# Attention and a gated MLP on one core: output transfers moved from SyncE's queue to ScalarE's, and one block of the attention matrix turned by VectorE only from the ninth pair on

## The chip, the cores and the metric

The kernel runs on one core of a Trainium2 chip. The metric is the device time of one execution in microseconds. A core has five engines, each with its own queue that is worked off in order: TensorE (PE in the profile; its weight loads are listed as PEld), VectorE (DVE), ScalarE (ACT), GpSimd (POOL) and SyncE (SP), which here only issues transfers. A transfer can be issued by SP or by ACT; it then runs beside the engines, and those who need it wait for a semaphore.

## The reference

Eight batches of eight heads, sequence 576, head size 64: causal attention with a decay per position, and behind it an MLP with a spatial gate.

```python
scores = scale * np.matmul(q, k.transpose(0, 1, 3, 2))
decay = cum[:, :, :, None] - cum[:, :, None, :]
scores = np.where(causal, -1000000000.0, scores + decay)
scores = scores - np.max(scores, axis=-1, keepdims=True)
attn = np.exp(scores)
attn = attn / (np.sum(attn, axis=-1, keepdims=True) + 1e-09)
x = np.matmul(attn, v)                      # then heads side by side: (8, 576, 512)
...
h = np.maximum(x @ w_in, 0.0)
u, v = (h[..., :d_ff // 2], h[..., d_ff // 2:])
v_n = (v - mu) / np.sqrt(var + 1e-06)
v_s = np.einsum('ts,bsd->btd', w_spatial, v_n) + b_spatial[None, :, None]
return ((u * v_s) @ w_out).astype(np.float32)
```

## The kernel before, in words

The heads are taken in pairs: 32 pairs P = 0 to 31, four to a batch (PPB = 4). A batch's attention (`attention`, L695) and a batch's MLP (`moe`, L724) are generators; the loop at L854 runs the MLP of batch b beside the attention of batch b + 1 and keeps the two level by the numbers `t_attn` and `t_moe` (L836). Batch 0's attention runs alone at the start, in `first` (L514). A scheduler with a model of time then fixes the order of each engine's queue; on the chip that order is kept.

**A pair.** PE makes the scores against 128 keys at a time (L328). DVE adds the decay and takes the row's minimum (L308), ACT makes the exponentials and their sum (L339), POOL divides by the sum (L316; for pairs 5 to 7 it is ACT, L314). The result is in the tiles `tt`, one per head, queries on the partitions. For the product with v it must stand the other way round, in `e`, in blocks c = 0 to 3 of 128 keys. Blocks 1 to 3 are turned by PE (L413, four, three, two or one pieces of 128 x 128) and copied out of PSUM by DVE and ACT in turn (L404). **Block 0 is moved** (`move`, L442): DVE turns it in pieces of 32 x 32 into `mid` (L449, one instruction per head), and SP issues 16 transfers of 32 KB (L456) that set the pieces on the right partitions of `e`, or of a second tile `ea` for every other pair. The matmuls on such a block (`spread`, L483) read it in its scattered order; the others are L475. Pairs 0 to 3 turn all four blocks on PE; from pair 4 on block 0 is moved.

**The MLP.** Per batch 576 rows: matmuls with w_in, norm, spatial product, gate (L803 to L807), and the last product with w_out in `w_out_tile` (L818): four tiles of 128 rows per batch, two after each half of the sequence, and behind every second batch one tile more with 64 rows of each of two batches. PE makes a tile in 12 matmuls into one of two PSUM buffers `ps`; ACT copies it to the SBUF tile `o` (L831), and it is sent out (L833). There is one buffer `o`: the next copy waits until the transfer before has landed. The first 64-row half of the tile behind every second batch, and all 128-row tiles, go out on SP's queue, the other half on ACT's.

**Loads.** SP also issues the loads: scores' inputs `qk_t` (L239), the decay rows `dk` (L251) and `dt` (L253), `vraw` (L293) for one pair ahead, and in batch 1's stretch the weights `w` in pieces (L125), which ACT, DVE and POOL split into a rounded part and a rest (L130 to L143). POOL masks each `dk` and `dt` after it has landed (L279 to L285).

**Semaphores of transfers.** The framework gives the transfers of both queues eight semaphores in turn (DMAHW0 to DMAHW7 below). A transfer is issued only when the one eight places before it in the program's order has landed, whichever queue that one is on.

Of the kernel before, what the change touches and what calls it, by code (L numbers as in the profile page):

```python
# [22 lines left out]
NB = 4  # L23
# [2 lines left out]
TOFF = (0, 128, 384, 768)  # L26
RSTEP = 384
ROFF = tuple(RSTEP * i for i in range(4))
MOVED = (0,)
HALVES = ((0, 256), (256, 320))  # L30
QK = 640 + S
EOFF = (0, 640, 1280, 1088, 576)


def f32(ap):
    return ap.bitcast(F32)
# [3 lines left out]
def attn_gmlp_kernel(ctx: ExitStack, tc: tile.TileContext, qk, v, f, w_in, w_sp, b_sp, w_out, out):  # L40
# [7 lines left out]
    B = out.shape[0]  # L48
    PPB = NPAIR // B
# [8 lines left out]
    V, A, G, T, SY = nc.vector, nc.scalar, nc.gpsimd, nc.tensor, nc.sync  # L58
# [125 lines left out]
    tt = [cst.tile([128, 3 * RSTEP + TL], F32, name=f"tt{h}") for h in range(2)]  # L184
# [4 lines left out]
    def turn(P):  # L189

        if P not in own:
            own[P] = tt, tl
            if P < PPB and P % 2:
                tl2 = wk.tile([128, 640], F32, name="tl2", tag="xh", bufs=6)
                G.memset(tl2[:, S:640], 0.0)
                own[P] = [ws_[0].tile([128, 1280], F32, name=f"t2{h}", bufs=1) for h in range(2)], tl2
        return own[P]
# [11 lines left out]
    def bank(n, piece=True):  # L209

        t = PS['s'].tile([128, 512], F32, name="sc", tag=f"sc{n}")
        if piece:
            banks.append(n)
        return t

    def in_one_piece(jobs, needs=()):

        was = None
        for job in jobs:
            if was is None:  # L220
                was = job()
                for j in [freed[n] for n in banks if n in freed] + list(needs):
                    behind(was, j, sync=True)
            else:
                with tc.high_priority():
                    i = job()
                behind(i, was)
                was = i
        banks.clear()

    def mm(o, l, r, st, sp):
        T.matmul(o, l, r, start=st, stop=sp)  # L232
# [58 lines left out]
    def prep_v(P):  # L291
        vraw = wk.tile([128, 5, 2, D], F32, name="vraw", tag="vraw")
        SY.dma_start(out=vraw, in_=v[P])  # L293
        vts[P] = vraw
# [96 lines left out]
    def e_tile(P):  # L391
        return e_all

    def e_first(P):

        return aside[P] if P in aside else e_all
# [10 lines left out]
    def turn_block(P, h, c):  # L407

        tt, _ = turn(P)
        n = 512 - 128 * c  # L410
        tp = bank(2 + c, False) if P < PPB and c > 1 else PS['t'].tile([128, 512], F32, name="tp")
        for i in range(c, NB):
            T.transpose(out=tp[:, (i - c) * 128:(i - c + 1) * 128],  # L413
                        in_=tt[h][:, off(P)[i] + 128 * c:off(P)[i] + 128 * c + 128], identity=ident)
        return lambda by=None: evac(P, e_tile(P)[:, h, EOFF[c]:EOFF[c] + n], tp[:, 0:n], by)
# [15 lines left out]

    def transposes(P, h):
        for c in range(NB):
            if c not in MOVED:
                turn_block(P, h, c)()
                yield 107 * (NB - c)

    def part(t, k, steps):

        return bass.AP(tensor=t.tensor, offset=t.offset, ap=[list(t.ap[0]), *steps])  # L440

    def move(P):  # L442

        tt, _ = turn(P)
        for c in MOVED:
            w = 128 - 32 * c
            mid = cst.tile([128, 2, 4, w], F32, name=f"mid{c}", tag=f"mid{c}")
            for h in range(2):
                V.transpose(out=part(mid[:, h], 0, [[32, NB - c], [w, 4], [1, 32]]),  # L449
                            in_=part(tt[h][:, ROFF[c] + 128 * c:], 0, [[RSTEP, NB - c], [32, 4], [1, 32]]))  # L450
            if P % 2:
                aside[P] = cst.tile([128, 2, 512], F32, name="ea")
            e = e_first(P)
            for g in range(4):
                for r in range(4):
                    copied.setdefault(P, []).append(SY.dma_start(  # L456
                        out=e[32 * r:32 * r + 32, :, EOFF[c] + w * g:EOFF[c] + w * g + w],
                        in_=mid[32 * g:32 * g + 32, :, r, :]))

    def transposes_tail(P):  # L460
        for cs, off, step in TAILS:
            turn_tail(P, cs, off, step)()
            yield 107 * len(cs)

    def attend(P, xh, xl):

        vt, e = vts[P], e_tile(P)
        moved = MOVED if P >= PPB else ()
        xb = 4 if P < PPB else 0
        x0, x1 = bank(xb), bank(xb + 1)  # L470
        jobs = []

        def product(x, s0, q0, q1, c, h, end):
            e0 = EOFF[c] - 128 * c
            return lambda: T.matmul(x[64 * h:64 * h + 64, q0 - s0:q1 - s0], vt[:, c, h, :],  # L475
                                    e[:, h, e0 + q0:e0 + q1], start=c == 0 and c not in moved, stop=c == end)

        def spread(x, m0, c, h, end):
            k0 = max(m0, c)
            n, w = m0 + 2 - k0, 128 - 32 * c  # L480
            src = part(e_first(P)[:, h, EOFF[c] + 32 * (k0 - c):], 0, [[w, 4], [32, n], [1, 32]])
            out = part(x[64 * h:64 * h + 64, 128 * (k0 - m0):], 0, [[32, 4], [128, n], [1, 32]])
            return lambda: T.matmul(out, vt[:, c, h, :], src, start=c == 0, stop=c == end)  # L483

        for c in range(NB + 1):
            for x, s0, q0, q1, end in ((x1, 256, max(256, 128 * c), S, NB), (x0, 0, 128 * c, 256, 1)):
                if c > end:
                    continue
                if c in moved:
                    jobs += [spread(x, s0 // 128, c, h, end) for h in range(2)]  # L490
                    if end < NB:
                        continue
                    q0 = TL
                jobs += [product(x, s0, q0, q1, c, h, end) for h in range(2)]
        in_one_piece(jobs, copied.pop(P))
        yield 2950
        for ps, s0, n in ((x0, 0, 256), (x1, 256, 320)):
            last[P, s0 // 256] = A.copy(xh[:, s0:s0 + n], ps[:, 0:n])
        yield 0
        for ps, s0, n in ((x0, 0, 256), (x1, 256, 320)):  # L500
            freed[xb + s0 // 256] = V.tensor_tensor(out=xl[:, s0:s0 + n], in0=ps[:, 0:n], in1=f32(xh[:, s0:s0 + n]),  # L501
                                               op=ALU.subtract)
        yield 0
# [191 lines left out]
    def attention(b):  # L695
        for P in range(b * PPB, (b + 1) * PPB):
            nxt = P + 1 < NPAIR
            prep_v(P)
            if nxt:
                list(prep(P + 1))  # L700
                mask(P + 1)
            if P == PPB:
                move(P)
            for h in range(2):
                yield from transposes(P, h)
            if nxt:
                yield from scores(P + 1)
            yield from transposes_tail(P)
            if nxt:
                yield from scores_tail(P + 1)  # L710
            yield from product(P)
# [106 lines left out]
    def w_out_tile(b, ghi, glo, dst):  # L818
        ps = acc(b)
        n = 0  # L820
        for j in range(NJ):
            for l, r in ((ghi, woh), (ghi, wol), (glo, woh)):
                mm(ps, l[j], r[:, j, :], n == 0, n == 3 * NJ - 1)
                n += 1
            yield 648
        tag, bufs = ("vx", 2) if b == B - 1 and nps[0] % 3 else ("o", 1)
        o = mo.tile([128, DM], F32, name="o", tag=tag, bufs=bufs)
        if b == B - 1 and nps[0] % 3 == 1:
            V.tensor_copy(o, ps)
        else:  # L830
            A.copy(o, ps)  # L831
        for bb, tok, p0, np_ in dst:
            (SY if p0 == 0 else A).dma_start(out=out[bb, tok:tok + np_, :], in_=o[p0:p0 + np_, :])  # L833


    t_attn, t_moe = 33600.0, 52500.0  # L836

    def step(gen, done, t):
        try:
            return done + next(gen) / t, True  # L840
        except StopIteration:
            return round(done), False

    with tc.tile_pool(name="ws", bufs=2) as ws, tc.tile_pool(name="p0s", bufs=1, space=PSUM) as p0s, \
# [4 lines left out]
        da, on = 1.0, False  # L849
# [4 lines left out]
    for b in range(B):  # L854
        gm = moe(b)
        dm, mon = 0.0, True
        while mon:
            while da < min(B, b + 1 + LEAD + dm):
                if not on:
                    gen, on = attention(int(round(da))), True  # L860
                da, on = step(gen, da, t_attn)
            dm, mon = step(gm, dm, t_moe)


# [41 lines left out]
```

## Time and profile before

| | us |
|---|---|
| three runs | 803.22, 805.36, 809.61 (median 805.36) |
| the profiled execution: its time | 804.17 |
| its span, first to last instruction | 802.4 |
| PE busy | 741.0 (92%) |
| DVE busy | 466.6 (58%) |
| ACT busy | 395.3 (49%) |
| POOL busy | 369.1 (46%) |

Mean granted clock of PE over the span: 0.979 of full speed. A busy PE is not a PE at its peak, since matmuls overlap and their ends are modelled; but PE's idle time and what ended it can be read directly. The shares are averages over stages: batch 0's attention alone (to about 74 us), batch 1's attention beside batch 0's MLP (to about 166 us), then six stretches of some 95 us, and the last MLP alone.

### The profile page before, as it was taken

How to read it: one execution, taken by the hardware profiler on the slowest of the kernel's cores; microseconds unless marked ns; L12 is line 12 of the kernel's file. 1: busy time of each engine (PE TensorE's matmuls, PEld its weight loads, DVE VectorE, ACT ScalarE, POOL GpSimd, SP SyncE). 2: the span in 40 equal slices, each digit the busy share in tenths (PEclk: the TensorE clock that was granted, in tenths of full speed). 3: DMA queues.
4: the chain of work that ended last, by engine and by line, in shares of the span. 5: the costliest groups of instructions: out<-in, count | busy, mean ns of one | idle time of the engine just before them, and what ended most of it. 6: DMA issues, size and time to landing. Idle time of an engine off the chain costs nothing.

```text
span 802.4 us, 15003 instructions
## 1 busy us (share of the span) xinstructions
PE 741.0 (92%) x4812; PEld 589.2 (73%) x4813; DVE 466.6 (58%) x1537; ACT 395.3 (49%) x1106; POOL 369.1 (46%) x682
## 2 busy tenths in 40 slices
PE   8778799599999899999899979999889989999997
PEld 4456577477888678886787757977678857888896
DVE  6896898745745457555655527555575535752332
ACT  7855678554644346445544345444364433642331
POOL 3985744454624365433634516344553435531241
PEclk9999999899999999999999989999999999999999
DMA  7746355544325433344233432344433443212001
GB/s 231 219 166 174 85 148 160 154 131 137 106 78 135 132 114 110 120 133 134 73 104 115 134 127 75 106 117 134 150 103 115 112 125 106 81 45 66 27 1 66
DMA packets 70160, 93.21 MB, mean 116 GB/s; under 512 B 11329, under 2 KB 44097, under 8 KB 70082
## 3 DMA queue, kind: packets, MB, share of 16 engines
q1 hardware_dynamic: 69762, 91.74, 38.9%
q8 instruction: 38, 0.62, 0.3%
q10 hardware_dynamic: 320, 0.52, 0.3%
q14 instruction: 40, 0.33, 0.1%
HBM read 67.78 MB, written 9.75 MB: 97 GB/s over the span
## 4 chain that ended last, share of the span: by engine, by line
PE 46%; SPq 10%; POOL 9%; DVE 6%; issue 5%; DMA 5%; ACT 4%; POOLq 0%; ACTq 0%; DVEq 0%
PE ps L232 28%; SPq L456 10%; POOL tt L316 6%; PE sc L328 5%; PE sc L232 4%; DMA out_dram<-o 3%; PE sc L475 3%; PE tp L413 2%; PE tp L232 2%; PE sc L483 2%; DVE tt L308 1%; DVE vx L758 1%; DVE mid L449 1%; DMA dk<-rows_d 1%; PE tp L423 1%
## 5 line engine op out<-in xcount | busy, mean ns | idle before, releaser
L339 ACT ACTIVATE tt<-tt,nm 128x384 f32<-128x384 f32 (+1 forms) x240 | 133.4, 558 | 58.8 <-DVE nm L308 56.7
L807 POOL TENSOR_TENSOR gl<-u,gh 128x256 fp32r<-128x256 f32 (+1 forms) x64 | 51.5, 806 | 162.6 <-ACT gh L806 160.8
L316 POOL TENSOR_SCALAR tt<-tt,sm 128x128 f32<-128x128 f32 x192 | 99.8, 539 | 44.3 <-DVE sm L355 42.8
L308 DVE CUSTOM_DVE_ANT_1 tt<-sc,dk 128x256 f32<-128x256 f32 (+1 forms) x120 | 65.5, 553 | 57.5 <-PE sc L328 40.9
L328 PE MATMUL sc<-qk_t 64*128 64x128 f32 (+3 forms) x512 | 88.5, 465 | 7.9 <-DVE xl L501 5.8
L232 PE MATMUL ps<-xh,winh 128*128 128x256 f32 (+1 forms) x232 | 74.7, 323 | 7.3 <-ACT vx L753 4.8
L475 PEld LDWEIGHTS sc<-e,vraw 128*64 128x64 f32 x784 | 55.6, 138 | 32.4 <-issue 5.7
L232 PE MATMUL ps<-winh,xh 128*128 128x512 f32 x148 | 64.0, 433 | 16.1 <-ACT o L831 15.0
L475 PE MATMUL sc<-e,vraw 128*64 128x320 f32 (+4 forms) x784 | 73.3, 324 | 5.5 <-ACT tl L627 4.3
L232 PE MATMUL ps<-sph,vnh 128*128 128x256 f32 (+1 forms) x240 | 76.6, 319 | 0.0
L404 ACT COPY e<-tp 128x384 f32<-128x384 f32 (+2 forms) x120 | 45.6, 380 | 55.0 <-PE tp L413 24.7
L413 PE MATMUL tp<-ident,tt 128*128 128x128 f32 x364 | 67.4, 280 | 5.2 <-ACT e L404 3.1
L404 DVE COPY e<-tp 128x384 f32<-128x384 f32 (+2 forms) x128 | 57.9, 455 | 22.9 <-PE tp L413 20.6
L232 PE MATMUL ps<-sph,vnl 128*128 128x256 f32 (+1 forms) x240 | 70.6, 294 | 0.0
L232 PE MATMUL ps<-spl,vnh 128*128 128x256 f32 (+1 forms) x240 | 70.6, 294 | 0.0
L232 PE MATMUL ps<-xl,winh 128*128 128x256 f32 (+1 forms) x232 | 69.6, 300 | 0.0
L232 PE MATMUL ps<-xh,winl 128*128 128x256 f32 (+1 forms) x232 | 69.3, 299 | 0.0
L328 PEld LDWEIGHTS sc<-qk_t 64*128 64x128 f32 x512 | 45.5, 191 | 30.9 <-DVE xl L501 7.1
L413 PEld LDWEIGHTS tp<-ident,tt 128*128 128x128 f32 x364 | 46.0, 142 | 25.2 <-issue 4.8
L449 DVE STREAM_TRANSPOSE mid<-tt 128x512 f32<-128x512 f32 x56 | 39.7, 708 | 37.0 <-POOL tt L316 31.1
L232 PE MATMUL ps<-winl,xh 128*128 128x512 f32 x148 | 60.3, 408 | 0.0
L308 DVE CUSTOM_DVE_ANT_0 tt<-sc,dk 128x384 f32<-128x384 f32 (+1 forms) x120 | 49.7, 418 | 10.6 <-PE sc L328 9.6
(218 smaller groups left out, 1818.5 us busy)
## 6 DMA issues: line engine op xcount, KB each, us to landing
qk_t<-in_dram SPq DMA_DIRECT2D x32, 608.0 KB, 5.5
dk<-rows_d SPq DMA_DIRECT2D x58, 320.0 KB, 4.6
vraw<-in_dram SPq DMA_DIRECT2D x32, 320.0 KB, 3.1
dt<-rows_d SPq DMA_DIRECT2D x58, 144.0 KB, 3.2
out_dram<-o SPq DMA_DIRECT2D x32, 256.0 KB, 2.2
e<-mid SPq DMA_DIRECT2D x224, 32.0 KB, 1.9
ea<-mid SPq DMA_DIRECT2D x224, 32.0 KB, 1.9
w<-in_dram SPq DMA_DIRECT2D x16, 256.0 KB, 3.3
```

The lines of the kernel that those rows point to most:

```text
L232: T.matmul(o, l, r, start=st, stop=sp)
L308: return V.tensor_tensor_reduce(out=out, in0=ps, in1=dec, scale=-0.125, scalar=3.0e38, op0=ALU.add, op1=ALU.min, accum_out=acc_)
L316: G.tensor_scalar(out=t, in0=t, scalar1=r, scalar2=1.0, op0=ALU.mult, op1=ALU.mult)
L328: return lambda: T.matmul(ps[:, c:c + n], qk_t[p, n - 128:n], qk_t[p, 640:640 + n], start=True, stop=True)
L339: last["exp", P, h, i] = A.activation(t, t, AF.Exp, bias=nm, scale=-1.0, accum_out=sm)
L404: copied.setdefault(P, []).append(by(out, ps))
L413: T.transpose(out=tp[:, (i - c) * 128:(i - c + 1) * 128], in_=tt[h][:, off(P)[i] + 128 * c:off(P)[i] + 128 * c + 128], identity=ident)
L449: V.transpose(out=part(mid[:, h], 0, [[32, NB - c], [w, 4], [1, 32]]), in_=part(tt[h][:, ROFF[c] + 128 * c:], 0, [[RSTEP, NB - c], [32, 4] ...
L456: copied.setdefault(P, []).append(SY.dma_start(out=e[32 * r:32 * r + 32, :, EOFF[c] + w * g:EOFF[c] + w * g + w], in_=mid[32 * g:32 * g + ...
L475: return lambda: T.matmul(x[64 * h:64 * h + 64, q0 - s0:q1 - s0], vt[:, c, h, :], e[:, h, e0 + q0:e0 + q1], start=c == 0 and c not in move ...
L483: return lambda: T.matmul(out, vt[:, c, h, :], src, start=c == 0, stop=c == end)
L807: G.tensor_tensor(out=gl[j][:, 0:nt], in0=g, in1=f32(gh[j][:, 0:nt]), op=ALU.subtract)
```

## The change

Two things. An output transfer is issued by ACT, in the queue that holds the copy to `o`, except in the last batch, where whole tiles stay on SP. And block 0 is moved only for pairs P >= 8; pairs 4 to 7 turn it on PE, as pairs 0 to 3 do. With that, the second tile `ea` goes to the even pairs and not the odd ones, the first of them being pair 8, and the pacing number of the attention that runs beside batch 0's MLP is 37000 and not 33600.

```diff
-MOVED = (0,)
...
     def transposes(P, h):
         for c in range(NB):
-            if c not in MOVED:
+            if c not in moved(P):
                 turn_block(P, h, c)()
                 yield 107 * (NB - c)
...
+    def moved(P):
+
+        return (0,) if P >= 2 * PPB else ()
...
         tt, _ = turn(P)
-        for c in MOVED:
+        for c in moved(P):
...
-            if P % 2:
+            if P % 2 == 0:
                 aside[P] = cst.tile([128, 2, 512], F32, name="ea")
...
-        moved = MOVED if P >= PPB else ()
+        away = moved(P)
...
-                if c in moved:
+                if c in away:
                     jobs += [spread(x, s0 // 128, c, h, end) for h in range(2)]
...
-            if P == PPB:
-                move(P)
...
         for bb, tok, p0, np_ in dst:
-            (SY if p0 == 0 else A).dma_start(out=out[bb, tok:tok + np_, :], in_=o[p0:p0 + np_, :])
+            (SY if p0 == 0 and b == B - 1 else A).dma_start(out=out[bb, tok:tok + np_, :], in_=o[p0:p0 + np_, :])
...
-    t_attn, t_moe = 33600.0, 52500.0
+    t_first, t_attn, t_moe = 37000.0, 33600.0, 52500.0
...
-                da, on = step(gen, da, t_attn)
+                da, on = step(gen, da, t_attn if b else t_first)
```

The changed kernel's line numbers are one lower than the kernel's before up to L433, and one to three higher behind it.

**ACT's queue at the end of an odd batch (batch 3).** `o<-ps` is the copy of an output tile, `tp` and `xh` belong to the attention beside it; in brackets stands what an instruction waits for by semaphore. Before:

```order
L498 CAST xh<-sc 128x320 [waits PE_49]
L831 COPY o<-ps 128x512 [waits DMAHW0_49,PE_49,Activation_49]
L404 COPY e<-tp 128x128 [waits PE_49]
L339 ACTIVATE tt_82,sm<-tt_82,nm 128x384 [waits DVE_49]
L339 ACTIVATE tt_82,sm<-tt_82,nm 128x256 [waits DVE_49,Pool_49]
L339 ACTIVATE tt_82,sm<-tt_82,nm 128x128 [waits DVE_49]
L831 COPY o<-ps 128x512 [waits DMAHW5_49,Activation_49]
L404 COPY e<-tp 128x256 [waits PE_49]
```

The same place in the changed kernel:

```order
L501 CAST xh<-sc 128x320 [waits PE_49]
L832 COPY o<-ps 128x512 [waits DMAHW2_49,PE_49]
L834 DMA out_dram<-o 128x512 [waits DMAHW5_49,Activation_49]
L403 COPY e<-tp 128x128 [waits PE_49]
L338 ACTIVATE tt_82,sm<-tt_82,nm 128x384 [waits DVE_49]
L832 COPY o<-ps 128x512 [waits DMAHW5_49]
L338 ACTIVATE tt_82,sm<-tt_82,nm 128x256 [waits DVE_49,Pool_49]
L834 DMA out_dram<-o 128x512 [waits DMAHW3_49,Activation_49]
```

The transfer now stands directly behind its copy, or one instruction behind it. Counted back eight places, the first transfer waits for a load `dt`, the second for the sixth of the 16 transfers of a move.

**SP's queue at the same place.** Before, and then in the changed kernel:

```order
L251 DMA dk<-rows_d 128x640
L253 DMA dt<-rows_d 64x576
L456 DMA e<-mid_5706 32x2x128 x16
L833 DMA out_dram<-o 128x512
L293 DMA vraw<-in_dram 128x640
L253 DMA dt<-rows_d 64x576
L833 DMA out_dram<-o 128x512
L833 DMA out_dram<-o 64x512
```

```order
L238 DMA qk_t<-in_dram 128x1216
L252 DMA dt<-rows_d 64x576 x2
L459 DMA ea<-mid_5668 32x2x128 x16
L292 DMA vraw<-in_dram 128x640
L250 DMA dk<-rows_d 128x640 x2
```

The output transfers stood behind the 16 of a move and are gone from the queue; both `dt` loads now stand ahead of the move.

**SP's queue in batch 1's stretch**, from pair 6 to pair 8's loads. Before, and then in the changed kernel:

```order
L125 DMA w_1727<-in_dram 128x2x256
L456 DMA e<-mid_1561 32x2x128 x16
L125 DMA w_1740<-in_dram 128x2x256
L125 DMA w_1753<-in_dram 128x2x256
L125 DMA w_1766<-in_dram 128x2x256
L251 DMA dk<-rows_d 128x640 x2
L239 DMA qk_t<-in_dram 128x1216
L253 DMA dt<-rows_d 64x576 x2
```

```order
L124 DMA w_1728<-in_dram 128x2x256
L252 DMA dt<-rows_d 64x576 x2
L292 DMA vraw<-in_dram 128x640
L250 DMA dk<-rows_d 128x640 x2
L238 DMA qk_t<-in_dram 128x1216
L252 DMA dt<-rows_d 64x576 x2
```

The move and three weight loads stood between the load before and pair 8's `dk`; now no weight load stands directly ahead of it, and no move.

## Rows read from the trace of the kernel before

**Rows 1.** The view of waits, PE alone: what its queue stood for, us in total, times, the longest (the three largest).

```profile
PE ps L232 <- ACT o L831: 15.0, 6, 4.6
PE sc L328 <- DVE xl L501: 5.8, 4, 2.4
PE ps L232 <- ACT vx L753: 5.8, 3, 2.4
```

**Rows 2.** The timeline of ACT near the end of batch 3's MLP: start us, length us, engine, line, operation, and in brackets the idle time before it and what ended it.

```profile
458.69 0.59 ACT L831 COPY o<-ps 128x512 f32<-128x512 f32 x1 [0.71 <-ACT xh L498]
...
469.38 0.58 ACT L831 COPY o<-ps 128x512 f32<-128x512 f32 x1 [6.45 <-DMA out_dram<-o]
...
472.24 0.58 ACT L831 COPY o<-ps 128x512 f32<-128x512 f32 x1 [0.53 <-DMA out_dram<-o]
```

**Rows 3.** The timeline of SP's queue in the same stretch.

```profile
453.59 0.50 SPq L253 DMA_DIRECT2D dt<-rows_d  x1
455.60 11.41 SPq L456 DMA_DIRECT2D e<-mid  x16
467.11 0.53 SPq L833 DMA_DIRECT2D out_dram<-o  x1
...
468.16 0.50 SPq L253 DMA_DIRECT2D dt<-rows_d  x1
```

**Rows 4.** The timeline of PE: the places at which it waited for that copy for over a microsecond, the first matmul of the next batch's MLP each time.

```profile
279.62 0.57 PE L232 MATMUL ps<-winh,xh 128*128 128x512 f32 x1 [2.48 <-ACT o L831]
375.44 0.50 PE L232 MATMUL ps<-winh,xh 128*128 128x512 f32 x1 [1.25 <-ACT o L831]
470.02 0.80 PE L232 MATMUL ps<-winh,xh 128*128 128x512 f32 x1 [4.63 <-ACT o L831]
568.27 0.50 PE L232 MATMUL ps<-winh,xh 128*128 128x512 f32 x1 [2.60 <-ACT o L831]
659.70 0.79 PE L232 MATMUL ps<-winh,xh 128*128 128x512 f32 x1 [3.79 <-ACT o L831]
```

**Rows 5.** The chain of waits, the same 12 matmuls behind four of these places: start us, length us.

```profile
279.62 4.61 PE ps L232 x12
...
375.44 3.03 PE ps L232 x12
...
470.02 5.08 PE ps L232 x12
...
659.70 5.49 PE ps L232 x12
```

**Rows 6.** The table by windows: stretch, its length, busy us (and count) of PE, PEld, DVE, ACT, POOL, then the granted clock of PE, the share of the DMA engines, GB/s.

```profile
470.00:475.20 5.20, 5.18 (x14) 3.85 (x16) 0.00 (x0) 2.37 (x9) 0.24 (x1) 0.57 0.44 138
...
153.60:157.00 3.40, 3.36 (x15) 2.37 (x16) 2.90 (x6) 1.15 (x3) 2.67 (x4) 0.50 0.21 48
```

**Rows 7.** The view of the tile `o`: its issues and copies with their lengths (ns, least, median, most), ACT's wait for it (us, times), and the time from issue to landing.

```profile
L833 SPq DMA_DIRECT2D out_dram<-o x36: 332/344/544, 166.6 to 798.4; - x36
...
L833 ACTq DMA_DIRECT2D out_dram<-o x4: 488/489/586, 282.4 to 798.3; - x4
...
  DMA out_dram<-o: 45.7, 17
...
DMA to landing us min/median/max: 2.0/2.2/6.4
```

**Rows 8.** The table by windows in batch 1's stretch, columns as in rows 6.

```profile
130.00:140.00 10.00, 8.73 (x62) 6.77 (x60) 9.80 (x37) 6.32 (x22) 4.69 (x7) 1.00 0.28 69
...
74.00:166.00 92.00, 75.88 (x478) 57.55 (x475) 72.64 (x238) 61.36 (x174) 45.16 (x74) 0.94 0.50 137
...
143.00:154.00 11.00, 4.70 (x36) 3.10 (x33) 6.54 (x21) 7.81 (x20) 3.44 (x8) 0.83 0.77 199
```

**Rows 9.** Timelines in that stretch: SP's loads for pair 8 behind a move, POOL's mask and the weight split behind it, the last score reduction of pair 7 on DVE and the DVE instruction that waited.

```profile
139.85 1.54 SPq L125 DMA_DIRECT2D w<-in_dram  x3
141.49 0.89 SPq L251 DMA_DIRECT2D dk<-rows_d  x2
...
147.96 0.41 POOL L279 TENSOR_SCALAR_AFFINE_SELECT dk<-dk 128x256 f32<-128x256 f32 x1 [5.49 <-DMA dk<-rows_d]
...
140.87 0.68 DVE L308 CUSTOM_DVE_ANT_1 tt<-sc,dk 128x512 f32<-128x512 f32 x1
...
151.18 0.42 DVE L135 SCALAR_TENSOR_TENSOR w<-w,wa 128x256 uint32<-128x256 uint32 x1 [3.50 <-POOL w L140]
```

**Rows 10.** The groups of instructions by line and shape: count, busy us, mean ns (the first from batch 1's stretch alone, the others from the whole span), and one row of PE's timeline with five pieces turned in a row.

```profile
L449 DVE STREAM_TRANSPOSE mid<-tt 128x512 f32<-128x512 f32 x8 | 5.6, 702 | 2.7 <-POOL tt L316 2.7
...
L404 DVE COPY e<-tp 128x384 f32<-128x384 f32 x68 | 36.9, 543 | 1.9 <-PE tp L423 1.9
...
L404 DVE COPY e<-tp 128x256 f32<-128x256 f32 x32 | 13.4, 418 | 20.1 <-PE tp L413 20.1
...
L404 DVE COPY e<-tp 128x128 f32<-128x128 f32 x28 | 7.9, 283 | 0.9 <-PE tp L413 0.5
...
L404 ACT COPY e<-tp 128x512 f32<-128x512 f32 x8 | 4.6, 574 | 0.0
...
79.77 0.71 PE L413 MATMUL tp<-ident,tt 128*128 128x128 f32 x5
```

**Rows 11.** The view of waits, SP's queue: what it stood for, us in total, times, the longest.

```profile
SPq L253 <- DVE nm L308: 91.5, 26, 5.2
```

More of the change, by code (lines that the diff above doesn't have):

```diff
@@ L433, in transposes, with part @@
         for c in range(NB):
-            if c not in MOVED:
+            if c not in moved(P):
                 turn_block(P, h, c)()
                 yield 107 * (NB - c)
-    def part(t, k, steps):
+    def moved(P):
+        return (0,) if P >= 2 * PPB else ()
+    def part(t, steps):
         return bass.AP(tensor=t.tensor, offset=t.offset, ap=[list(t.ap[0]), *steps])
@@ L448, in move @@
             for h in range(2):
-                V.transpose(out=part(mid[:, h], 0, [[32, NB - c], [w, 4], [1, 32]]),
-                            in_=part(tt[h][:, ROFF[c] + 128 * c:], 0, [[RSTEP, NB - c], [32, 4], [1, 32]]))
-            if P % 2:
+                V.transpose(out=part(mid[:, h], [[32, NB - c], [w, 4], [1, 32]]),
+                            in_=part(tt[h][:, ROFF[c] + 128 * c:], [[RSTEP, NB - c], [32, 4], [1, 32]]))
+            if P % 2 == 0:
                 aside[P] = cst.tile([128, 2, 512], F32, name="ea")
@@ L475, in product @@
             return lambda: T.matmul(x[64 * h:64 * h + 64, q0 - s0:q1 - s0], vt[:, c, h, :],
-                                    e[:, h, e0 + q0:e0 + q1], start=c == 0 and c not in moved, stop=c == end)
+                                    e[:, h, e0 + q0:e0 + q1], start=c == 0 and c not in away, stop=c == end)
         def spread(x, m0, c, h, end):
@@ L480, in spread @@
             n, w = m0 + 2 - k0, 128 - 32 * c
-            src = part(e_first(P)[:, h, EOFF[c] + 32 * (k0 - c):], 0, [[w, 4], [32, n], [1, 32]])
-            out = part(x[64 * h:64 * h + 64, 128 * (k0 - m0):], 0, [[32, 4], [128, n], [1, 32]])
+            src = part(e_first(P)[:, h, EOFF[c] + 32 * (k0 - c):], [[w, 4], [32, n], [1, 32]])
+            out = part(x[64 * h:64 * h + 64, 128 * (k0 - m0):], [[32, 4], [128, n], [1, 32]])
             return lambda: T.matmul(out, vt[:, c, h, :], src, start=c == 0, stop=c == end)
```

## The prediction, made before the changed kernel ran

> **What bounds the kernel now.** I read the page first (PE is busy for 741.0 of 802.4 us), then PE's own waits, then the timelines around the longest of them. The largest single wait of PE is for ACT's copy of an output tile: 15.0 us in six places [rows 1]. They all stand where one batch's MLP ends and the next begins, and at five of them PE loses 1.25 to 4.63 us [rows 4].
>
> The largest shows why. ACT copies one output tile at 458.69, and then waits 6.45 us before it can copy the next, because the single buffer `o` has not been sent [rows 2]. It was ready for sending at 459.3. But SP was inside a move: 16 issues from 455.60 on, 11.41 us, so the output transfer was issued only at 467.11 [rows 3]. It landed 2.2 us later, as such transfers do [rows 7]. PE waited for the PSUM buffer that ACT could not empty. So the output was late by SP's issue time, not by its own length.
>
> A long stop costs a second time. The 12 matmuls behind it take 3.03 us at 375.44, but 4.61, 5.08 and 5.49 behind three of the other stops [rows 5]; at 470 us the granted clock was 0.57 of full speed, a stretch mostly at the lower of the two levels, 1.2 and not 2.4 GHz [rows 6].
>
> The second weak place is batch 1's stretch, where weights are split beside the attention. In 92 us PE is busy for 75.9, and 6.3 of the 16.1 idle us lie between 143 and 154; DVE is at 9.80 of 10 us just before that hole [rows 8]. In the hole POOL stands 5.49 us before the mask of pair 8's `dk`, a weight split is queued behind it, and DVE stands 3.50 us for that split [rows 9]. The load was issued at 141.49, behind a move and three weight loads that began at 139.85; but it could not have gone before DVE had read the old `dk` for the last time, at 140.87 to 141.5 [rows 9].
>
> **The change, part by part.**
>
> *A. Outputs leave SP's queue.* The order of ACT puts the issue one or two places behind the copy. From the end of a copy it is then 0.49 us of issue and 2.2 us to landing [rows 7], some 2.7 us, until the buffer is free, and not the 10.1 us from 459.3 to 469.4 [rows 2]. PE needs 3.03 us for a tile's 12 matmuls [rows 5] and has two PSUM buffers, so the copies keep up. I take all 15.0 us away [rows 1]; the bounds are 15.0 and 7.5, the latter if other waits in the same places take half of it.
>
> *B. Clock.* Without the three long stops the 12 matmuls behind them take 3.03 each: 1.58 + 2.05 + 2.46 = 6.1 us [rows 5]. If A comes only by half, stops of about 2 us are left, and the row behind 375.44 shows that a short one is not followed by the low clock: so B holds in that case too, at least in part.
>
> *C. Issues on ACT.* 31 of the 36 transfers that SP issued come over, 31 x 0.49 = 15.1 us of ACT's time [rows 7]; the four rows on ACT are of half the size, so this is an estimate. SP gets back 31 x 0.34 = 10.7 us [rows 7]. ACT is idle half the time and gets back most of the 45.7 us that it stood for `o` [rows 7], which is the cover. Without that cover the whole 15.1 us lie on the path. Between 0 and 15.1 I take 2, near the lower end, because the issue follows a copy and the next thing on ACT usually waits for PE or DVE anyway.
>
> *D. Batch 1 without moves.* Gone: 8 DVE turns, 5.6 us [rows 10], and 64 issues in four moves, some 11 us of SP's time each [rows 3]. Added on PE: 4 pairs x 2 heads x 4 pieces = 32 turned pieces; five take 0.71 us [rows 10], so at most 0.14 each, 4.5 us. The matmuls on block 0 stream the same columns in either form. Added copies out of PSUM: by the order of the copies, all eight of block 0 (512 wide, 0.574 each, 4.6 us) fall to ACT, and of the others DVE gets four more of 384 and of 128 and four fewer of 256, 4 x (0.543 + 0.283 - 0.418) = 1.6 us [rows 10]. So DVE is relieved by 4.0 us, while ACT (61.4 busy of 92 [rows 8]) gets less than 4.6 more. DVE was the engine that held pair 8's load back, so I let that load and the hole behind it come 4 us earlier: -4. The bounds: -6.3, if the hole vanishes, and +4.5, if PE's new pieces all lie on the path and nothing is won. PE has 16.1 idle us in this stretch to hide them [rows 8]; if POOL's queue still stands before a `dk`, that cover is worth little, and DVE and PE wait as now.
>
> *E. The pacing number and the swap of `e` and `ea`:* nothing. The number makes room for the 32 pieces; the swap lets pair 8, the first moved, write a tile that pair 7 does not read. What hides both is the plain fact that no wait for a moved block is among PE's three largest [rows 1].
>
> *Sum against the profiled execution:* 802.4 - 15.0 - 6.1 + 2 - 4 = 779.3 us of span, and 1.8 us around it (804.17 - 802.4): **781 us**. The median of the three runs, 805.36, lies 0.15% above that execution; I make no correction for it.
>
> **A rule that speaks against it.** In the rows, SP needs 11.41 us to issue a move whose next transfer lands in 2.2 us [rows 3, 7], so here the issuing is the long part. The Trainium skill says otherwise in "DMA: Bandwidth & Descriptors", section "Issuing engines are not separate DMA queues": transfers started by several engines share the same 16 DMA engines, and a second issuer saves only the time to initiate, usually small beside the transfer itself. By that rule A and B would not come, which is the second rival.
>
> **The rivals.**
>
> 1. *The stop comes back in another form.* With the output on time, the next thing that PE lacks at a batch's end could be the attention's own chain: the next largest waits are for `xl` on DVE and `vx` on ACT, 5.8 us each [rows 1]. Then A gives 7.5 and B 3: 802.4 - 7.5 - 3 + 4 - 2 + 1.8 = 796. For it: several of these waits follow the same places. Against: PE's work is ready there, only the PSUM buffer lacks.
>
> 2. *The transfer is late whichever queue issues it*, since the move's 16 transfers fill the DMA engines. Then only D and SP's freed time are left: 802.4 - 4 + 2 + 1.8 = 802. Against: the transfer landed 2.2 us after a late issue, and the DMA engines were at 0.44 then [rows 6, 7].
>
> 3. *ACT stands where SP stood: slower.* A transfer may be issued only when the one eight places before it has landed. For ACT's that is a load `dt` or the fifth or sixth transfer of a move, both on SP. SP stood 91.5 us in all before `dt`, for DVE [rows 11]. If `dt` or the move is late by more than some 3 us at the copy, ACT stands with all behind it, exponentials included. The five stops average 2.95 us (14.75 / 5 [rows 4]); at all 14 places (two in each of seven batches) that is 41 us in place of 15.0 + 6.1: 781 + 41 = 822. It decides from 3 us of lateness on; at half of it the time is 802. Against: at 458.69 `dt` had been issued 5.1 us before, and the sixth of the move's transfers, at 11.41 / 16 = 0.71 us each, at about 459.9 [rows 2, 3], ahead of the second copy.
>
> **How the numbers follow.** What a measurement can tell from no change is about 1%, 8 us. My forecast, A to D with the bounds of D and C's lower half (771 to 790): 0.60; 771 leaves some room for the two 5.8 us waits of rival 1 to shrink. Rival 1 (790 to 797): 0.20. Rival 2 and a mild form of rival 3 (797 to 813): 0.11. Rival 3 in full (above 813): 0.06. Below 771: 0.03. So the range is 771 to 797, which holds 0.80; faster by over 1% is 0.60 + 0.20 + 0.03 = 0.83, within 1% 0.11, slower 0.06.
>
> **What will show it.** A: ACT's wait for `out_dram<-o` falls from 45.7 to under 20 us, and PE's wait for ACT's `o` from 15.0 to under 3. B: no 12 matmuls above 4 us at a batch's first tile. C: the issue rows of ACT read about 0.5 us x 35. D: the idle time of PE in batch 1's stretch falls below 16 us in spite of 4.5 us more work, and DVE's turns there are gone. Rival 1 would show as larger waits for `xl` or `vx`; rival 2 as landings of 5 us and more; rival 3 as ACT's queue standing before its issues. The forecast is wrong if the stops at the batches' ends remain, or if batch 1's stretch is longer than 92 us.

## The result, and the profile after

The changed kernel takes **780.93 us** (median of 4 runs, 777.98 to 783.95), the kernel before beside it 804.59: a ratio of **0.9695 [0.9637, 0.9754]**. The forecast was 781, with 771 to 797 as its range. In the profiled execution the span is 780.2 us in place of 802.4.

The waits of PE, the first and some further down, us in total, times, longest (the rows of before are [rows 1]):

```profile
PE tp L412 <- DVE e L403: 8.5, 5, 3.9
...
PE ps L231 <- ACT vx L754: 3.9, 4, 1.5
...
PE sc L327 <- DVE xl L504: 0.9, 3, 0.4
...
PE ps L231 <- ACT o L832: 0.6, 2, 0.3
```

The wait for ACT's copy of `o` has gone from 15.0 to 0.6 us. The two next of before are smaller too, `xl` 5.8 to 0.9 and `vx` 5.8 to 3.9. But another now leads the list: DVE's copy `e`, 8.5 us. In the kernel before that wait was 1.3:

```profile
PE tp L413 <- DVE e L404: 1.3, 1, 1.3
```

The view of the tile `o`, which answers to [rows 7]:

```profile
L834 ACTq DMA_DIRECT2D out_dram<-o x35: 333/339/854, 157.3 to 775.9; - x35
...
L834 SPq DMA_DIRECT2D out_dram<-o x5: 332/383/544, 760.5 to 776.2; - x5
...
  DMA out_dram<-o: 9.8, 8
...
DMA to landing us min/median/max: 2.0/2.3/5.9
```

The transfer itself is as long as before (median 2.3 us, before 2.2). ACT's wait for it fell from 45.7 us to 9.8. An issue of a whole tile, 256 KB, takes ACT 0.339 us, and not the 0.49 of its earlier, half as large ones.

The timeline of ACT at the end of batch 3's MLP, the place of [rows 2]:

```profile
453.25 0.59 ACT L832 COPY o<-ps 128x512 f32<-128x512 f32 x1 [0.45 <-PE ps L231]
...
453.87 0.34 ACTq L834 DMA_DIRECT2D out_dram<-o  x1
...
456.61 0.59 ACT L832 COPY o<-ps 128x512 f32<-128x512 f32 x1 [0.18 <-DMA out_dram<-o]
...
459.52 0.59 ACT L832 COPY o<-ps 128x512 f32<-128x512 f32 x1 [1.41 <-DMA out_dram<-o]
```

And SP's queue in the same stretch, for [rows 3]:

```profile
449.71 10.90 SPq L459 DMA_DIRECT2D ea<-mid  x16
```

SP is still in a move, from 449.71 to 460.61, while ACT sends the outputs beside it. The copies begin 3.36 and 2.91 us after one another; before it was 10.69 and 2.86.

What ended last, by engine, in the chain of waits, before and then after:

```profile
PE 46%; SPq 10%; POOL 9%; DVE 6%; issue 5%; DMA 5%; ACT 4%; POOLq 0%; ACTq 0%; DVEq 0%
```

```profile
PE 67%; POOL 6%; DVE 4%; ACT 3%; DMA 2%; issue 2%; POOLq 0%; SPq 0%; DVEq 0%; ACTq 0%
```

SP's issuing, a tenth of the chain before, has left it.

Behind three of the long stops, the 12 matmuls of a batch's first tile took 4.61, 5.08 and 5.49 us [rows 5], with a granted clock of 0.57 at the second of them [rows 6]. In the changed kernel the first tile of the same three batches takes 3.00 to 3.14 us at 1.00, the upper of the two levels (columns as in [rows 6]). That gives 5.9 us.

```profile
279.32:282.32 3.00, 3.00 (x16) 2.50 (x15) 2.05 (x9) 2.46 (x7) 0.75 (x2) 1.00 0.65 190
459.39:462.53 3.14, 3.14 (x15) 2.57 (x14) 1.07 (x5) 2.31 (x8) 0.00 (x0) 1.00 0.54 98
639.28:642.42 3.14, 3.14 (x15) 2.57 (x14) 1.08 (x5) 2.46 (x8) 0.00 (x0) 1.00 0.45 105
```

Batch 1's stretch, by windows (columns as in [rows 6]; the first and the last line answer to [rows 8]):

```profile
74.00:166.00 92.00, 80.47 (x507) 62.59 (x503) 69.23 (x217) 61.16 (x165) 46.41 (x75) 0.96 0.39 120
...
143.00:154.00 11.00, 11.00 (x50) 8.10 (x47) 6.98 (x29) 8.20 (x27) 5.15 (x8) 0.80 0.14 46
```

The hole at 143 to 154 is filled (50 matmuls in place of 36, at a granted clock of 0.80), and PE's idle time in the 92 us is 11.5 in place of 16.1. Whether that is worth time at the end, the experiments tell.

### The profile page after: what moved, and what is told of

It is laid out like the page before. It is cut to its first block, busy times and chain, and to the rows that moved or that the text cites. A ratio compares the mean times of both kernels' runs of the same rounds, so it can differ in the third digit from the quotient of the medians.

```text
span 780.2 us, 14894 instructions
## 1 busy us (share of the span) xinstructions
PE 737.7 (95%) x4828; PEld 587.0 (75%) x4829; DVE 467.5 (60%) x1533; ACT 400.9 (51%) x1110; POOL 367.3 (47%) x682
## 4 chain that ended last, share of the span: by engine, by line
PE 67%; POOL 6%; DVE 4%; ACT 3%; DMA 2%; issue 2%; POOLq 0%; SPq 0%; DVEq 0%; ACTq 0%
PE ps L231 39%; PE sc L327 7%; PE sc L231 5%; PE sc L478 5%; PE tp L412 4%; PE sc L486 2%; POOL tt L315 2%; PE tp L231 2%; PE tp L422 1%; POOL mv L758 1%; DVE vx L759 1%; DMA dt<-rows_d 1%; ACT tt L338 1%; POOL vnl L763 1%; ACT vnh L761 1%
## 5 line engine op out<-in xcount | busy, mean ns | idle before, releaser
L338 ACT ACTIVATE tt<-tt,nm 128x384 f32<-128x384 f32 (+2 forms) x240 | 133.6, 558 | 66.1 <-DVE nm L307 62.1
L412 PE MATMUL tp<-ident,tt 128*128 128x128 f32 x396 | 71.0, 282 | 10.7 <-DVE e L403 8.5
L478 PE MATMUL sc<-e,vraw 128*64 128x320 f32 (+4 forms) x800 | 75.9, 329 | 5.5 <-ACT tl L630 4.3
L231 PE MATMUL ps<-xh,winh 128*128 128x256 f32 (+1 forms) x232 | 73.0, 315 | 4.4 <-ACT vx L754 3.3
L403 DVE COPY e<-tp 128x384 f32<-128x384 f32 (+2 forms) x132 | 59.7, 455 | 23.7 <-PE tp L412 19.7
L403 ACT COPY e<-tp 128x256 f32<-128x256 f32 (+2 forms) x124 | 48.7, 393 | 47.4 <-PE sc L478 25.0
L412 PEld LDWEIGHTS tp<-ident,tt 128*128 128x128 f32 x396 | 48.5, 142 | 31.7 <-issue 8.5
L807 ACT CAST gh<-u 128x256 fp32r<-128x256 f32 (+1 forms) x64 | 27.4, 431 | 74.3 <-DVE u L804 36.6
L452 DVE STREAM_TRANSPOSE mid<-tt 128x512 f32<-128x512 f32 x48 | 34.1, 711 | 45.5 <-POOL tt L315 38.5
L231 PE MATMUL ps<-winl,xh 128*128 128x512 f32 x148 | 58.2, 393 | 0.0
```

What stands on the lines that cost most here:

```text
L338: last["exp", P, h, i] = A.activation(t, t, AF.Exp, bias=nm, scale=-1.0, accum_out=sm)
L403: copied.setdefault(P, []).append(by(out, ps))
L412: T.transpose(out=tp[:, (i - c) * 128:(i - c + 1) * 128], in_=tt[h][:, off(P)[i] + 128 * c:off(P)[i] + 128 * c + 128], identity=ident)
L452: V.transpose(out=part(mid[:, h], [[32, NB - c], [w, 4], [1, 32]]), in_=part(tt[h][:, ROFF[c] + 128 * c:], [[RSTEP, NB - c], [32, 4], [1, ...
L807: A.copy(gh[j][:, 0:nt], g)
```

## The experiments

Two theories were tried against each other. **The buffer theory**: all of the gain comes from the output buffer being free in time (terms A and B), whoever sends it. Its rivals: the gain comes from SP's queue or from the issuer as such, or from batch 1 (term D).

**1. Only the transfers move.** The kernel before with the one line of the change:

```diff
-            (SY if p0 == 0 else A).dma_start(...
+            (SY if p0 == 0 and b == B - 1 else A).dma_start(...
```

> Only the output transfers move to ACT; pairs 4 to 7 keep their moves. My theory (the one buffer `o` is held by a transfer that stands behind SP's moves): the gain of parts A to C alone, 17 to 20 us, so 785 to 788 us; PE's wait for ACT's `o` below 1 us, ACT's wait for the transfer below 15 us. Rival (the gain comes from batch 1's stretch without moves, the stops at the batches' ends were covered): within 6 us of the kernel before.

Measured: 781.27 us, ratio 0.9728 [0.9686, 0.977]. This line alone is the whole gain. Its PE, on the page:

```profile
PE 735.1 (94%) x4813; PEld 588.2 (76%) x4813; DVE 469.1 (60%) x1537; ACT 399.3 (51%) x1106; POOL 368.5 (47%) x682
```

In a span of 778.4 us PE idles 43.3 us, 18.1 less than before, and is busy 5.9 us less. PE's wait for `o` (0.3 us) and ACT's for the transfer (13.2) came as expected; the time lies 4 us below the 785 to 788 of the theory, and far from the rival's.

**2. Only batch 1 without moves.** The changed kernel with the transfers back on SP. It keeps the new pacing number and the swap of the tiles too, so it tries terms D and E together:

```diff
-            (SY if p0 == 0 and b == B - 1 else A).dma_start(...
+            (SY if p0 == 0 else A).dma_start(...
```

> Only pairs 4 to 7 lose their moves; whole output tiles stay on SP. My theory: part D alone, 2 to 6 us faster than before (798 to 802), PE's wait for ACT's `o` stays near 15 us. Rival: 15 us or more faster. If the two parts do not add up to the 24 us of the whole, one of them changes what the other is worth.

Measured: 802.32 us, ratio 0.999 [0.9962, 1.0017]. No difference that can be told from noise. PE's wait for ACT's `o` stays, 14.7 us. The window of batch 1's stretch in this kernel (before: [rows 8]):

```profile
74.00:166.00 92.00, 82.31 (x521) 63.79 (x518) 69.65 (x218) 61.98 (x165) 47.67 (x77) 0.97 0.40 123
```

PE issues 521 matmuls in place of 478 there and idles 9.7 us in place of 16.1. But this is for the most part another order of the same work. Three places on ACT show it, each before and then here: the first copy of an output tile (batch 0's MLP), the last two `xh` of batch 1's attention, and the first `gh` of batch 2's MLP.

```profile
166.01 0.56 ACT L831 COPY o<-ps 128x512 f32<-128x512 f32 x1
156.03 0.56 ACT L832 COPY o<-ps 128x512 f32<-128x512 f32 x1
...
171.95 0.70 ACT L498 CAST xh<-sc 128x256 fp32r<-128x256 f32 x2
186.07 0.71 ACT L501 CAST xh<-sc 128x256 fp32r<-128x256 f32 x2
...
325.24 0.40 ACT L806 CAST gh<-u 128x256 fp32r<-128x256 f32 x1 [1.84 <-DVE u L803]
326.68 0.40 ACT L807 CAST gh<-u 128x256 fp32r<-128x256 f32 x1 [1.84 <-DVE u L804]
```

The MLP of batch 0 runs 10.0 us ahead of its place before, batch 1's attention ends 14.1 us behind its own, and two batches later nothing of a lead is left: this execution is 1.4 us behind. The added pieces show in the groups, before and then here:

```profile
L413 PE MATMUL tp<-ident,tt 128*128 128x128 f32 x364 | 67.4, 280 | 5.2 <-ACT e L404 3.1 <-DVE e L404 1.3 <-POOL tt L316 0.2
```

```profile
L412 PE MATMUL tp<-ident,tt 128*128 128x128 f32 x396 | 71.1, 278 | 6.3 <-DVE e L403 4.4 <-ACT e L403 1.2 <-POOL tt L315 0.5
```

The 32 pieces cost PE 3.7 us. Over the span PE is busy for 5.6 us more and idle for 6.8 us less, and the two cancel but for 1.2. Where the other 1.9 us of busy time come from is not shown.

**3. Transfers on SP, but two buffers.** The kernel before, tiles by turns in two buffers:

```diff
-        tag, bufs = ("vx", 2) if b == B - 1 and nps[0] % 3 else ("o", 1)
+        tag, bufs = ("vx", 2) if b == B - 1 and nps[0] % 3 else (("o", "o2")[nps[0] % 2], 1)
```

> The kernel before with a second buffer for the output tile, taken in turn; all transfers stay where they were. My theory (what costs is that ACT must wait for a late transfer before it can copy): most of the 15 + 6 us comes without touching the queue, 786 to 792 us; PE's wait for ACT's `o` below 4 us, while the transfers are issued as late as before, behind the move. Rival (what helps is that SP's queue is freed of the transfers and of its waits for ACT, so that loads and moves come earlier): within 4 us of the kernel before.

Measured: 795.27 us, ratio 0.9896 [0.9845, 0.9947], less than half of the gain, and outside both what was expected and the rival's range. PE's direct wait for ACT's `o` is off the list, as expected; the stops come back in another form. The timelines of ACT, SP and PE around the end of a batch, in this order:

```profile
281.39 0.59 ACT L831 COPY o<-ps 128x512 f32<-128x512 f32 x1 [2.80 <-DMA out_dram<-o]
```

```profile
267.84 10.27 SPq L456 DMA_DIRECT2D e<-mid  x16
278.21 1.80 SPq L833 DMA_DIRECT2D out_dram<-o  x2
```

```profile
294.46 0.50 PE L232 MATMUL ps<-winh,xh 128*128 128x512 f32 x1 [2.15 <-ACT vx L753]
```

Two outputs now queue behind one move (x2 at 278.21), and the third tile of a run of three needs the first one's buffer: ACT stands 2.80 us before that copy, and 3.16 and 2.80 us at two more such places (465.72, 650.61). Some 13 us behind each of the three, PE stands 2.15 to 2.60 us for ACT's `vx`; that wait is 10.0 us in all here, and 4.4 in experiment 1. That the one brings on the other is argued from their places; experiment 4 tries it.

**4. Transfers on SP, three buffers.**

```diff
+        tag, bufs = ("vx", 2) if b == B - 1 and nps[0] % 3 else (("o", "o2", "o3")[nps[0] % 3], 1)
```

> The kernel before with three buffers for the output tile in turn, all transfers on SP behind the moves as before. My theory (two buffers fell short only because the third tile of an odd batch again had to wait for a transfer behind the move): PE's 2.15, 2.60 and 2.39 us at those three places go, and the whole gain of moving the outputs is reached without moving them, 0.970 to 0.978. Rival (SP's queue freed of the outputs is worth the rest): it stays at 0.985 to 0.990 as with two buffers.

Measured: 782.65 us, ratio 0.9741 [0.9702, 0.978]. That is the whole gain, with the issues still in SP's queue behind the moves. The view of `o`:

```profile
L833 SPq DMA_DIRECT2D out_dram<-o x36: 332/377/559, 166.0 to 775.9; - x36
...
  DMA e<-mid: 3.5, 3
```

SP issues 36 transfers as before, and ACT's wait for `out_dram<-o` is no longer on the list. With it PE's stops at the three places of experiment 3 are gone, 7.1 us in all, as the matmuls that stood there show in experiment 3 and then here:

```profile
L232 PE MATMUL ps<-winh,xh 128*128 128x512 f32 x148 | 61.5, 415 | 7.1 <-ACT vx L753 7.1
```

```profile
L232 PE MATMUL ps<-winh,xh 128*128 128x512 f32 x148 | 62.4, 421 | 0.0
```

So two buffers are one too few for SP's queue, and neither another issuer nor a relieved SP is needed for the gain. PE stood because a single buffer had to be sent before it could be filled again.

**5 and 6. Both cures together.** Two buffers with the transfers on ACT: in the changed kernel, and in the kernel before, which keeps the moves in batch 1. The edit of the first is experiment 3's line; the second has both lines:

```diff
-        tag, bufs = ("vx", 2) if b == B - 1 and nps[0] % 3 else ("o", 1)
+        tag, bufs = ("vx", 2) if b == B - 1 and nps[0] % 3 else (("o", "o2")[nps[0] % 2], 1)
...
-            (SY if p0 == 0 else A).dma_start(...
+            (SY if p0 == 0 and b == B - 1 else A).dma_start(...
```

> The changed kernel with a second buffer for the output tile, taken in turn. My theory: the 9.8 us that ACT still waits for the buffer lie beside PE's work (PE waits 0.6 us), so within 3 us of the changed kernel (778 to 784). Rival (ACT is now the engine that holds others up): 4 to 8 us faster than the changed kernel.

> Outputs on ACT and two buffers, moves for pairs 4 to 7 kept. It stands to the changed kernel with two buffers (0.967) as the outputs alone (0.973) stand to the changed kernel (0.9695). My theory (batch 1 without moves is worth 2 to 4 us at most): 0.967 to 0.972. Rival (it is worth nothing, or costs): equal to or below the changed kernel by 2 us or more.

Measured: 776.68 us, 0.967 [0.9623, 0.9717], and 776.42 us, 0.9656 [0.9629, 0.9683]. In both the rival came and the theory did not, the second time by a little. The first is 4.2 us faster than the changed kernel's 780.93, though the intervals of the two ratios overlap. The second stands beside the changed kernel itself (781.36, see 7): 4.9 us less, and the two intervals do not meet. So the 9.8 us that ACT still waited for the buffer did not lie wholly beside PE's work. That the two agree says once more that batch 1 without moves is worth nothing that can be measured here. The second, the kernel before with two edited lines, has the lowest median of the case, level with the first.

What the second buffer takes away shows in PE's waits. For DVE's copy `e` and ACT's `vx` they were 8.5 and 3.9 us in the changed kernel; with two buffers they are

```profile
PE tp L412 <- DVE e L403: 5.2, 3, 4.0
...
PE ps L231 <- ACT vx L754: 2.2, 4, 0.8
```

Of the 5.2 us 4.0 are the stop of batch 1's stretch. Behind 160 us neither of the two kernels has a stop of PE above 0.9 us.

**7. The price of an issue on ACT.** The changed kernel again, and one that sends each tile as two transfers of 64 rows:

```diff
-            (SY if p0 == 0 and b == B - 1 else A).dma_start(out=out[bb, tok:tok + np_, :], in_=o[p0:p0 + np_, :])
+            for r in range(p0, p0 + np_, 64):
+                (SY if p0 == 0 and b == B - 1 else A).dma_start(out=out[bb, tok + r - p0:tok + r - p0 + 64, :], in_=o[r:r + 64, :])
```

> The changed kernel once more, so that the others of this call stand beside it on one chip: 0.9695 of the kernel before, within 0.5%.

> The changed kernel with each 128-row output sent as two transfers of 64 rows: 28 issues more on ACT, the same bytes, no copy more. My theory (an issue on ACT lies beside PE's work): within 2 us of the changed kernel. Rival (ACT's issues lie on the path): 28 x 0.34 to 0.49 = 9.5 to 13.7 us slower than the changed kernel.

Measured: 781.36 us, 0.9723 [0.969, 0.9756], and 784.5 us, 0.9757 [0.9733, 0.9782]. The doubled one issues, in its view of `o`:

```profile
L835 ACTq DMA_DIRECT2D out_dram<-o x63: 473/484/855, 155.2 to 776.5; - x63
```

28 more issues on ACT, each 0.484 us and no longer 0.339, take 28 x 0.484 + 35 x (0.484 - 0.339) = 18.6 us more of ACT's queue and cost 3.1 us at the end (784.5 - 781.36). That is above the 2 us of the theory and far below the rival's 9.5; the intervals overlap, so this is a size and not a proof. Nor is it the price of issuing alone, since the second issue also frees the buffer later: PE's wait for ACT's `o`, in the changed kernel again and then in the doubled one, is

```profile
PE ps L231 <- ACT o L832: 0.2, 1, 0.2
```

```profile
PE ps L231 <- ACT o L832: 3.6, 4, 2.0
```

and this 3.4 us more is as much as the whole cost. What an issue on ACT costs beside that stays open.

## Why the prediction was right

The direction, the range and the mechanism of A and B hold. That the time is met to 0.1 us is luck: A, B and C together were some 3 to 4 us too small, and D some 2 to 3 us too large.

- **A (outputs leave SP's queue, -15.0): right, and a little too small.** PE's wait for `o` fell from 15.0 to 0.6 us. Experiment 4 shows the mechanism: with enough buffers the same gain comes on SP. What the term left out is that the waits behind the stops also shrink: in experiment 1 `xl` falls from 5.8 to 3.3 and `vx` from 5.8 to 4.4. PE's idle time fell by 18.1 us there. Even so the cure is not whole. The 2.7 us until the buffer is free leave out the copy itself: from copy to copy it is 3.36 and 2.91 us in the rows above, about as long as PE's 3.03 for a tile. So ACT still stood 9.8 us, and a second buffer gave 4 to 5 us more (experiments 5 and 6).
- **B (clock, -6.1): right.** The three slow first tiles give back 5.9 us in the changed kernel, at a clock of 1.00. PE's whole busy time is 5.9 us less in experiment 1. The sentence beside it, that a short stop is not followed by the low clock, was too broad; see the last section.
- **C (issues on ACT, +2): open.** An issue takes 0.339 us, not 0.49, so the 31 take 10.5 us and not 15.1. What they cost on the path no run measures alone: in experiment 7 the cost goes with a buffer that is free later. A, B and C together were -19.1; experiment 1 measured -22.9 (781.27 - 804.14), or -21.9 by its ratio.
- **D (batch 1 without moves, -4): wrong.** Together with E it measured 0.999 [0.9962, 1.0017], so -0.8 us by the ratio and -1.8 by the medians, with both signs inside the interval and -4 (0.995) just outside. The step that failed is "so I let that load and the hole behind it come 4 us earlier: -4": it takes time won in one stretch for time won at the end. The cover was there. PE's idle time did fall, with the 32 pieces in the stretch, and the hole at 143 did go, as the prediction's own sign for it says. But the pieces are 3.7 us of work on the engine that bounds the kernel, batch 1's attention ended 14.1 us later while the MLP beside it came 10.0 us earlier, and two batches on PE's work was no further than before. How much of that is the pieces, the pacing number of E or a new stop, no run tells. In the changed kernel a stop now stands a little ahead of where the hole was; PE's timeline has

```profile
141.67 0.48 PE L412 MATMUL tp<-ident,tt 128*128 128x128 f32 x1 [3.90 <-DVE e L403]
142.07 2.93 PE L327 MATMUL sc<-qk_t 64*128 64x384 f32 x12
```

and the chain of waits before it runs through a weight split:

```profile
138.32 0.44 ACT wa L129
...
138.78 0.79 DVE wa L131
...
141.15 0.47 DVE e L403
```

DVE's copy `e`, for which PE stood, is queued behind five DVE instructions of that split and of `xl`. Experiment 2 has a stop of 3.37 us at 141.85 too.
- **E (nothing):** it was not tried alone. No wait for a moved block is on PE's list in the changed kernel, which fits the swap's part of it. Whether the pacing number has a part in the new order of batch 1's stretch is not shown.
- **Rival 1 (the stop comes back in another form)** is half there: `vx` and `e` now hold PE for 3.9 and 8.5 us. The 8.5 are mostly in three places, 3.90, 2.13 and 1.44 us. The first is batch 1's and thus term D's. The other two are A's: with two buffers (experiments 5 and 6) they are gone, as are the longer ones for `vx`.
- **Rival 2 (late whichever queue issues it)** falls with the landing time, 2.3 us in the median; at 453.87, in the middle of a move, ACT issues an output, and 2.74 us later it starts the next copy into the same buffer (456.61). The sentence of the Trainium skill cited for it ("DMA: Bandwidth & Descriptors", section "Issuing engines are not separate DMA queues") is borne out in one half: the transfers are no faster. The saved time to initiate was the part that mattered, because it was not one issue but the 16 ahead of it in SP's queue, 11.41 us [rows 3]. Experiment 4 shows the limit of even that: given buffers, those 11 us cost nothing that can be measured.
- **Rival 3 (ACT stands where SP stood)** did not come: in ACT's timeline none of the 35 issues starts more than 0.11 us behind the instruction before it. In the view of `o`, 0.9 us of standing ends with a move's transfer.

The signs named ahead held for A (0.6 under 3; 9.8 under 20), B (the 12 matmuls of the three first tiles take 3.00 to 3.14 us, under 4) and in form for D (idle 11.5 under 16); for C the row reads 0.339 x 35 and not 0.5. The sign against the forecast, a stretch of batch 1 longer than 92 us, cannot be read: its MLP ends earlier than before and its attention later. The lesson of D is that its sign could hold without its gain, since a stretch's idle time was counted and not the time by which the same work was done.

## What to carry to other kernels

When an engine stands before a buffer that "has not been sent", compare the time from issue to landing with the time from ready to issue: here 2.2 us against 8, so the queue ahead of the issue was late, not the transfer. Another issuer cures it, and so do enough buffers to outlast that queue (three here, where two gave less than half); both together gave the lowest time.
Work that is moved onto the bounding engine may fill a hole there and still win nothing: here 32 pieces went into a stretch with 16.1 idle us, the idle time fell, and the end did not move. Judge it by when the same instruction is reached some stretches later, not by the idle time or the count of matmuls inside the one stretch.

## What was not expected of the hardware

An issue's length depends on what is issued, and not as its size would have it: on ACT 0.339 us for 128 rows (256 KB), 0.484 us for 64 rows (128 KB), and on SP 0.595 us in the median for each 32 KB piece of a move (the 16 take 10.27 to 11.41 us in the rows shown, pauses included):

```profile
L459 SPq DMA_DIRECT2D ea<-mid x192: 587/595/1678, 186.9 to 687.6; - x192
```

Which stops are followed by the low clock is not told by [rows 5] alone. In the changed kernel the same 12 score matmuls take 2.93 us behind a stop of 3.90, 2.59 behind one of 2.13, and 1.57 behind one of 1.44. The last two, from PE's timeline:

```profile
388.55 0.52 PE L412 MATMUL tp<-ident,tt 128*128 128x128 f32 x3 [2.13 <-DVE e L403]
389.30 2.59 PE L327 MATMUL sc<-qk_t 64*128 64x384 f32 x12 [0.23 <-DVE xl L504]
```

```profile
570.05 0.52 PE L412 MATMUL tp<-ident,tt 128*128 128x128 f32 x3 [1.44 <-DVE e L403]
570.79 1.57 PE L327 MATMUL sc<-qk_t 64*128 64x384 f32 x12 [0.23 <-DVE xl L504]
```

The granted clock was 0.50, 0.67 and 1.00 of full speed in those stretches (141.70 to 146.70, 388.60 to 391.90, 570.00 to 572.40), where 0.50 is the lower of the two levels, 1.2 GHz. So a stop of about 2 us was paid for a second time here, by about 1 us, and the prediction's example of a harmless one [rows 4] was 1.25 us long. But length alone does not decide. In the kernel before, the stop of 2.48 us at 279.62 was followed by 4.61 us for the 12 matmuls [rows 4, 5], and the longer one of 2.60 at 568.27 [rows 4], whose matmuls [rows 5] leaves out, by 3.04 at the full clock. (The places at 375.44 and 568.27 are not the first matmuls of a batch's MLP, as [rows 4] has it, but a later tile's; those MLPs begin at 368.10 and 559.58.)

```profile
568.27:571.31 3.04, 3.04 (x13) 2.54 (x14) 1.95 (x8) 2.82 (x8) 0.93 (x3) 1.00 0.50 187
```

What else decides is not shown.
